# First-layer products of two neighbouring blocks in 512 columns, attention output in one PSUM bank instead of two

## The chip, the cores and the metric

The kernel runs on one core of a Trainium2 chip. The metric is the device time of one execution in microseconds (us). A core has five engines with a queue each: TensorE (PE in the profile, its weight loads PEld), VectorE (DVE), ScalarE (ACT), GpSimd (POOL) and SyncE (SP), which here issues most transfers. PSUM, into which TensorE writes, has eight banks of 128 partitions by 512 fp32 values.

## The reference

Three stages follow each other. A recurrent attention with decay makes 3072 rows of 384 values; a two-layer network with the same weights for all rows follows; then a routed layer with eight experts, which only rows with a positive skip score enter.

```python
f = 1 / (1 + exp(-f_logit))                       # 4 batches, 8 heads, 768 steps, 48 values
state = f[t] * state + outer(k[t], v[t])          # per head 48 x 48
y[t] = q[t] @ state
x = y.transpose(0, 2, 1, 3).reshape(3072, 384)
h = x @ w_in                                      # 384 x 2048
x = (h - tanh(h)) @ w_out                         # 2048 x 384
do = x @ w_skip > 0; e = argmax(x[do] @ w_gate)   # 8 experts, 384 x 1024 x 384
out = x; out[do] += gate * (relu(x @ w1[e]) @ w2[e])
```

## The kernel before, in words

**Units and blocks.** The rows are cut into 24 units of 128 rows (`u`: time chunk `c`, batch `b`); two units make a block of 256 rows (`blk`, 12 of them). `attend(u)` plans a unit's attention: `pl` (running sums of the decay, TensorE), `tk` and `tq` (transposes of k and q), `scores`, `mask` (DVE), `values`, the copies `out1` and `out2` (ACT), `renew` and `decay` of the state `S`. The transposed block then lies in `xT[blk]`, as a high part (`xhi`, ACT) and a low part (`xlo`, DVE). There are three such buffers (`AHEAD + 1`), and `xhi` of a block waits for the last first-layer product of the block three before (`lastG`).

**Attention on TensorE.** `scores` issues the 16 products `ps` of k and q (L511) and, for units 4 to 23, the 8 products of q with the state, which the code calls `recall` (L520). Heads come in four pairs `p` with two members `j`; member `j` has its state and its q on partitions 64j to 64j+47. The output `py` lies in two banks, one for each `j`. `side(p, j)` swaps the halves of the output for `p` of 2 and 3, so a recall of pair `p` and one of pair `p+2` use the four quarters of the 128 by 128 array between them: rows 0 or 64, columns 0 or 64. `values` adds the 8 products of the masked scores with v to `py` (L552) and makes the new state's part `pu` (L559). In the first chunk (units 0 to 3) the state is zero, and two products of 256 columns (L531) only set `py`.

**The two layers.** `gemm1(blk, f)` (step `G`) is one of 16 first-layer products of a block: nine matmuls of 128x256, three for each of three row groups (`whi` with both parts of x, `wlo` with the high part), L695. `tanh` (ACT, L702), `bend` (DVE, L707), `ghi` (ACT, L715) and `glo` (POOL, L721) follow, and `gemm2(blk, f)` (step `H`) adds six matmuls of 128x384 to the block's two accumulators `po` (L738). `H` stands two products behind `G` (`LAG`). After a block's last `H` its rows are copied out (`fin`), sent, and routed: nine dot products on DVE (L268), the choice, one small product `pp`, a scatter on POOL.

**What sets the order.** Blocks 0 to 9 are planned: every piece is a `Step` with an engine, a key, a cost and the PSUM buffers that it takes and gives. `in_order` lists the steps as a model of the engines would begin them, the first ones by the list `OPENING`, and they are emitted in that order, so each engine's queue is fixed. Blocks 10 and 11 are a hand-written loop of G, the routing steps, H. Eight experts close the program.

**PSUM before.** Four pools of two banks: `ph` (G's output), `po` (accumulators), `pa` (attention's short-lived tiles) and `yp` (both banks of `py`; block 1's accumulators too).

Of the kernel before, what the change touches and what calls it, by code (L numbers as in the profile page):

```python
# [97 lines left out]
def decay_attention_moe_kernel(  # L98
# [15 lines left out]
    P = 128  # L114
# [18 lines left out]
    FIRST, NJOIN, NPAY, SKEW = 6, 4, 6, 0  # L133
    EARLIEST, LEAD = -100, 32
# [284 lines left out]
    xT, xfs, dds = {}, {}, {}  # L419

    def side(p, j):

        return j if p < 2 else 1 - j
# [3 lines left out]
    def step(name, key, eng, cost, emit, *after, take=(), give=(), moved=0.0, lag=0.15):  # L427

        made[name] = x = Step(key, eng, cost, emit, after, take, give, moved, lag)
        steps.append(x)  # L430

    def attend(u):
# [13 lines left out]
        def at(pos):  # L446
            return (NF * blk - LEAD if u > FIRST - 1 else EARLIEST + 12 * blk) + 6 * half + pos
# [53 lines left out]

        def scores():
            kT, qT = m["kT"], m["qT"]
            ps = m["ps"] = [pa.tile([P, 512], F32, tag="pa", name=f"ps{u}_{j}") for j in range(2)]
            py = m["py"] = [yp.tile([P, 512], F32, tag="yp", name=f"py{u}_{j}") for j in range(2)]
# [10 lines left out]
            def recall(p):  # L516
                for j in range(2):
                    r = slice(64 * j, 64 * j + D)
                    o, w = 64 * side(p, j), (64, D)[side(p, j)]
                    nc.tensor.matmul(  # L520
                        py[j][o : o + w, p % 2 * P : p % 2 * P + P], lhsT=S[b][r, p, :w], rhs=qT[r, p],
                        start=(p % 2 == 0), stop=False,
                    )

            for p in range(2):
                score(p)
                if c:
                    recall(p)
                    recall(p + 2)
                else:  # L530
                    nc.tensor.matmul(  # L531
                        py[p][:64, : 2 * P], lhsT=S[b][:, 0].bitcast(BF16)[:, :64],
                        rhs=ones[:112, None, :].to_broadcast([112, 2, P]), start=True, stop=False,
                    )
                score(p + 2)
# [11 lines left out]
        def values():  # L547
            vt, py = loaded["v", u], m["py"]
            for p in range(NP):
                for j in range(2):  # L550
                    o = 64 * side(p, j)
                    nc.tensor.matmul(  # L552
                        py[j][o : o + D, p % 2 * P : p % 2 * P + P], lhsT=vt[:, 2 * p + j], rhs=m["A", j][:, p],
                        start=(c == 0 and o > 0 and p % 2 == 0), stop=(p % 2 == 1),
                    )
# [13 lines left out]

        def out1():  # L570
# [9 lines left out]
            py = m["py"]  # L580
            nc.scalar.activation(tm[:, half], py[1][:112, P : 2 * P], AF.Copy)
            nc.scalar.activation(xf[:112, 2, half], py[1][:112, :P], AF.Copy)

        def out2():
            nc.scalar.activation(
                xfs[blk][0][:112, :2, half], m["py"][0][:112, : 2 * P].rearrange("a (p t) -> a p t", p=2), AF.Copy
            )
# [34 lines left out]
        def xhi():  # L622
            x = xT[blk] = mpool.tile([P, KT, 2, 2 * P], F32R, tag="xT", name=f"xT{blk}", bufs=AHEAD + 1)
            nc.scalar.activation(x[:, :, 0], xfs[blk][0].rearrange("p k u t -> p k (u t)"), AF.Copy)
# [19 lines left out]
        step(("ck", u), at(1), "ACT", 0.59, copy4("k"), ("tk", u), ("scores", u - 2), give=((pk_in, f"k{u}"),))  # L644
        step(("tq", u), at(1.5), "PE", 0.44, turn4("q", qp4), ("mq", u), ("tk", u), take=((pk_in, f"q{u}"),), lag=0.25)
        step(("cq", u), at(1.5), "ACT", 0.59, copy4("q"), ("tq", u), ("scores", u - 2), give=((pk_in, f"q{u}"),))
        step(
            ("scores", u), at(2), "PE", 1.5 if c else 1.0, scores, ("ck", u), ("cq", u), ("decay", u - B), ("values", u - 1), 
            take=[("pa", f"s{u}{j}") for j in range(2)] + [("yp", f"y{u}{j}") for j in range(2)], lag=0.25,
        )  # L650
        for j in range(2):
# [4 lines left out]
        step(("values", u), at(3), "PE", 1.7 if u < FIRST else 1.3, values, ("mask", u, 1), ("v", u), take=(("pa", f"u{u}"),), lag=0.25)  # L656
        step(
            ("out1", u), at(3.5), "ACT", 0.6, out1, ("values", u), ("xlo", u - 1 - half) if blk > 1 else None, ("out2", u - 1),
            give=(("yp", f"y{u}1"),),
        )  # L660
        step(("out2", u), at(3.5), "ACT", 0.38, out2, ("out1", u), give=(("yp", f"y{u}0"),))
# [24 lines left out]
    po = {}  # L686

    def gemm1(blk, f):
        x = xT[blk]
        ph = ph_pool.tile([P, 2 * P], F32, tag="ph", name=f"ph{blk}_{f}")  # L690
# [6 lines left out]
        gt[blk, f] = ph  # L697
# [31 lines left out]
    def gemm2(blk, f, rows=(0, 1)):  # L729
        t = gt[blk, f]  # L730
        if f == 0:
            for s in range(2):
                home, tag, w = {1: (yp, "yp", 512)}.get(blk, (po_pool, "po", DM))
                po[blk, s] = home.tile([P, w], F32, tag=tag, name=f"po{blk}_{s}")[:, :DM]
        for s in rows:
            ss = slice(s * P, (s + 1) * P)
            for n, (a, w) in enumerate(((0, uhi), (0, ulo), (1, uhi))):
                nc.tensor.matmul(  # L738
                    po[blk, s], lhsT=t[:, a, ss], rhs=w[:, f], start=(f == 0 and n == 0), stop=(f == NF - 1 and n == 2)
                )  # L740
# [77 lines left out]
    def number():  # L818
        for at, n, begin in ((32, 32, (D * 7 - D + 32, 16)), (0, D, (0, 2 * D)), (96, 32, (D * 3 - 64 - D + 96, 16)), (64, D, (D * 4, 2 * D))):
            ids3 = rowid[at : at + n].rearrange("p (j i) -> p j i", i=KT)  # L820
            nc.gpsimd.iota(ids3, [[1, NWL], [NWL * begin[1], KT]], base=NWL * begin[0], channel_multiplier=NWL)
            if n == D:
                nc.gpsimd.iota(
                    ids3[:, :, KT - 1], [[1, NWL]], base=NWL * D * (1 if at else 5), channel_multiplier=NWL
                )
# [189 lines left out]
    def product2(g):  # L1015
        nonlocal routing
        blk, f = divmod(g - LAG, NF)
        first = (0,) if g - LAG >= NSLOT - SPLIT else (0, 1)
        gemm2(blk, f, first)
        if f == NF - 1:  # L1020
            finish(blk, first)
            if blk < NB - 1:
                for r in routing:
                    for _ in r:
                        pass
                routing = [late_route(2 * blk), late_route(2 * blk + 1)]
# [44 lines left out]
    for u in range(NU):  # L1071
        blk, half = divmod(u, 2)
        e = EARLIEST + 6 * u if u < FIRST else NF * blk - LEAD + 6 * half - 8
# [27 lines left out]
    slots = [(0, f) for f in range(NJOIN)] + [(1, f) for f in range(NJOIN - SKEW)]  # L1101
    for f in range(NJOIN, NF + SKEW):
        slots += [(b, f - SKEW * b) for b in range(2) if f - SKEW * b < NF]
    slots += [(b, f) for b in range(2, NB - AHEAD) for f in range(NF)]
    homes = {1: "yp"}
    for n, (b, f) in enumerate(slots):
        def do(fn, b=b, f=f):
            return lambda: fn(b, f)

        step(  # L1110
            ("G", n), n, "PE", 1.08, do(gemm1), ("xlo", 2 * b + 1), ("low", f // 2), ("G", n - 1), take=(("ph", f"g{n}"),), lag=0.25,
        )
        step(("T", n), n - 1000, "ACT", 0.39, do(tanh), ("G", n), ("glo", n - 2), ("ln", FIRST - 1))
        step(("bend", n), n - 1000, "DVE", 0.43, do(bend), ("T", n), give=(("ph", f"g{n}"),))
        step(("ghi", n), n - 1000, "ACT", 0.43, do(ghi), ("bend", n), ("H", n - LAG - 1))
        step(("glo", n), n - 1000, "POOL", 0.74, do(glo), ("ghi", n))
        if n == len(slots) - LAG:
            break_at = n
        if n < len(slots) - LAG:
            p = homes.get(b, "po")  # L1120
            step(
                ("H", n), n + LAG, "PE", 1.05, do(gemm2), ("glo", n), ("lou", f // 2), ("H", n - 1),
                ("values", FIRST - 1) if b in homes else None,
                take=[(p, f"o{b}{s}") for s in range(2)] if f == 0 else (), lag=0.25,
            )
            if f == NF - 1:
                for u in (2 * b, 2 * b + 1):
# [4 lines left out]
                    step(("out", u), n + LAG + 1, "SP", 0.45, (lambda u=u: finish2(u)), ("fin", u), moved=1.1)  # L1132
                    r = pieces(route(u))
# [10 lines left out]
        if f == NF - 1:  # L1144
# [10 lines left out]
    for g in range(NF * (NB - AHEAD), NSLOT + LAG):  # L1155
# [3 lines left out]
        for _ in range(3 if g >= NSLOT - NF else 2):  # L1159
# [412 lines left out]
```

## Time and profile before

| | |
|---|---|
| runs shown | 722.06, 721.72, 720.56 us; median 721.72 |
| the profiled execution | 720.9 us; span 718.9 us |
| TensorE busy | 691.1 us, 96% of the span, 6194 matmul records |
| VectorE, ScalarE, GpSimd busy | 68%, 51%, 42% |
| granted TensorE clock | 0.995 of full speed |
| chain that ended last | TensorE 75%, of it second-layer products 23%, first-layer products 23% |

A matmul's record holds its latency, so records overlap: what one matmul costs in a row of them is read from the distance between starts. An fp32 matmul of the attention leaves two records, one of the two layers (fp32r) leaves one. A row with "x8" is eight records that follow each other.

### The profile page before, as it was taken

The page shows a single profiled execution, that of the slowest core. Times are in us where ns is not written, and L with a number is a line of the kernel's source. Part 1 is how long each engine was busy: PE and PEld are TensorE (multiplying, and loading weights), DVE is VectorE, ACT ScalarE, POOL GpSimd, SP SyncE. Part 2 cuts the span into 40 slices and gives each one's busy share as a digit, 9 for nine tenths or more (in the row PEclk, how much of TensorE's full clock was granted, in tenths as well). Part 3 has the DMA queues.
Part 4 walks back from the last instruction along what each step waited for, and adds up shares of the span by engine and source line. Part 5 has one row for each costly group of instructions (what it writes and reads, how often), then busy time and mean ns, then how long its engine had stood idle before and what let it go on. Part 6 is the DMA issues. An engine that isn't in the chain of part 4 may idle for free.

```text
span 718.9 us, 16483 instructions
## 1 busy us (share of the span) xinstructions
PE 691.1 (96%) x6194; PEld 651.2 (91%) x6194; DVE 489.7 (68%) x1388; ACT 364.5 (51%) x882; POOL 300.5 (42%) x340
## 2 busy tenths in 40 slices
PE   7899989999999999999999999999999899999995
PEld 4578889999998999999999999999999789999995
DVE  3988987789669968668685774945585745555531
ACT  4867666546444564356546445444333435555530
POOL 4546444324244343443434344334443314555551
PEclk9999999999999999999999999999999999999998
DMA  9894345733121312312221220014002567666500
GB/s 221 224 258 133 116 170 144 253 75 63 46 45 48 72 34 72 58 50 46 63 62 29 59 44 14 24 59 157 6 35 91 192 216 232 216 214 215 175 16 24
DMA packets 147501, 76.75 MB, mean 107 GB/s; under 512 B 113288, under 2 KB 142617, under 8 KB 147286
## 3 DMA queue, kind: packets, MB, share of 16 engines
q1 hardware_dynamic: 142550, 64.18, 33.1%
q0 software_dynamic: 4768, 11.39, 4.5%
q8 instruction: 50, 0.82, 0.5%
q14 instruction: 37, 0.30, 0.1%
q10 hardware_dynamic: 96, 0.05, 0.0%
HBM read 61.60 MB, written 15.86 MB: 108 GB/s over the span
## 4 chain that ended last, share of the span: by engine, by line
PE 75%; DVE 9%; issue 5%; POOL 3%; ACT 3%; DMA 3%; SPq 0%; POOLq 0%; DVEq 0%; ACTq 0%
PE po L738 23%; PE ph L695 23%; PE eh L1224 8%; PE eo L1248 8%; PE ps L511 3%; DMA f<-in_f_logit_dram 3%; PE py L552 2%; POOL gs L721 2%; DVE scr L268 2%; PE eh L985 1%; PE pk L490 1%; PE py L520 1%; PE pu L559 1%; DVE th L707 1%; PE pq L490 1%
## 5 line engine op out<-in xcount | busy, mean ns | idle before, releaser
L721 POOL TENSOR_TENSOR gs<-th,gs 128x256 fp32r<-128x256 f32 x190 | 167.9, 887 | 233.6 <-ACT gs L715 214.7
L738 PE MATMUL po<-uhi,gs 128*128 128x384 f32 x768 | 232.3, 344 | 5.6 <-POOL gs L721 3.5
L695 PE MATMUL ph<-xT,whi 128*128 128x256 f32 x1152 | 219.7, 287 | 1.6 <-DVE th L707 1.3
L695 PEld LDWEIGHTS ph<-xT,whi 128*128 128x128 f32 x1152 | 184.2, 189 | 5.7 <-DVE th L707 2.8
L695 PE MATMUL ph<-xT,wlo 128*128 128x256 f32 x576 | 162.6, 282 | 0.0
L738 PEld LDWEIGHTS po<-uhi,gs 128*128 128x128 f32 x768 | 142.0, 189 | 12.0 <-POOL gs L721 6.4
L707 DVE TENSOR_TENSOR th<-ph,th 128x256 f32<-128x256 f32 x192 | 79.8, 418 | 85.2 <-ACT th L702 84.8
L268 DVE CUSTOM_DVE_ANT_0 scr<-pay,wb 128x384 f32<-128x384 f32 x198 | 128.8, 650 | 7.9 <-ACT pay L746 4.1
L715 ACT ACTIVATE gs<-th 128x256 fp32r<-128x256 f32 x192 | 79.5, 416 | 102.9 <-DVE th L707 100.5
L738 PE MATMUL po<-ulo,gs 128*128 128x384 f32 x384 | 129.2, 336 | 0.0
L702 ACT ACTIVATE th<-ph 128x256 f32<-128x256 f32 x192 | 72.4, 379 | 102.0 <-PE ph L695 66.9
L695 PEld LDWEIGHTS ph<-xT,wlo 128*128 128x128 f32 x576 | 109.4, 190 | 0.0
L738 PEld LDWEIGHTS po<-ulo,gs 128*128 128x128 f32 x384 | 73.1, 190 | 0.0
L1224 PE MATMUL eh<-xt,w 128*128 128x256 f32 x504 | 69.8, 283 | 0.0
L1248 PE MATMUL eo<-w,h 128*128 128x384 f32 x336 | 69.5, 342 | 0.0
L1224 PEld LDWEIGHTS eh<-xt,w 128*128 128x128 f32 x504 | 67.1, 188 | 0.4
L1248 PEld LDWEIGHTS eo<-w,h 128*128 128x128 f32 x336 | 56.5, 188 | 0.0
L1233 DVE SCALAR_TENSOR_TENSOR h<-eh,h 128x256 fp32r<-128x256 f32 x56 | 23.7, 422 | 46.1 <-ACT h L1232 46.1
L1232 ACT ACTIVATE h<-eh 128x256 fp32r<-128x256 f32 x56 | 21.5, 385 | 62.6 <-PE eh L1224 62.5
L780 POOL DMA_INDIRECT xs<-pay,dst x24 | 25.1, 1046 | 64.2 <-DVE sm L280 21.2
L352 POOL TENSOR_TENSOR w<-r,w 128x768 fp32r<-128x768 f32 x24 | 44.3, 1853 | 12.7 <-ACT w L351 12.7
L957 POOL DMA_INDIRECT out_dram<-yo,xa x16 | 15.9, 992 | 68.2 <-DVE yo L965 22.1
(194 smaller groups left out, 933.2 us busy)
## 6 DMA issues: line engine op xcount, KB each, us to landing
r<-in_moe_w_dram SPq DMA_DIRECT2D x56, 384.0 KB, 4.7
stgu<-in_moe_w_out_dram SPq DMA_DIRECT2D x4, 1536.0 KB, 6.3
f<-in_f_logit_dram SPq DMA_DIRECT2D x24, 192.0 KB, 3.3
out_dram<-pay SPq DMA_DIRECT2D x24, 192.0 KB, 3.5
k<-in_k_dram SPq DMA_DIRECT2D x22, 192.0 KB, 3.5
q<-in_q_dram SPq DMA_DIRECT2D x22, 192.0 KB, 3.1
v<-in_v_dram SPq DMA_DIRECT2D x22, 192.0 KB, 4.4
xs<-zrow SPq DMA_DIRECT2D x2, 1544.0 KB
```

The costliest lines, as they stand in the source:

```text
L268: nc.vector.tensor_tensor_reduce(out=scr, in0=x, in1=wb[:, n], scale=1.0, scalar=0.0, op0=ALU.mult, op1=ALU.add, accum_out=lg[:, n : n + 1])
L352: eng.tensor_tensor(lo, raw, hi.bitcast(F32), ALU.subtract)
L695: nc.tensor.matmul(ph, lhsT=w[:, i, fs], rhs=x[:, i, a], start=(n == 0), stop=(n == 3 * KT - 1))
L702: nc.scalar.activation(th, ph, AF.Tanh)
L707: nc.vector.tensor_tensor(th, ph, th, ALU.subtract)
L715: nc.scalar.activation(t[:, 0], th, AF.Copy)
L721: eng.tensor_tensor(t[:, 1], th, t[:, 0].bitcast(F32), ALU.subtract)
L738: nc.tensor.matmul(po[blk, s], lhsT=t[:, a, ss], rhs=w[:, f], start=(f == 0 and n == 0), stop=(f == NF - 1 and n == 2))
L780: nc.gpsimd.indirect_dma_start(xs[:, :], bass.IndirectOffsetOnAxis(ap=di, axis=0), pt[:, :], None, bounds_check=E * NT - 1, oob_is_err=False,)
L1224: nc.tensor.matmul(ph, lhsT=a1[:, w, i, f * P : (f + 1) * P], rhs=xt[:, i, a], start=(n == 0), stop=(n == 3 * KT - 1))
L1233: nc.vector.scalar_tensor_tensor(out=h[:, 1], in0=ph, scalar=0.0, in1=h[:, 0].bitcast(F32), op0=ALU.max, op1=ALU.subtract)
L1248: nc.tensor.matmul(eo[e, s], lhsT=h[:, a, ss], rhs=a2[:, w, f], start=(f == 0 and n == 0), stop=(f == NF2 - 1 and n == 2))
```

## The change

- From block 2 to block 9, a first-layer product is made for two neighbouring blocks at once: the nine matmuls have 512 columns, 256 of each block, and one weight load serves both. Blocks are offset by half a width: block 2 makes its products 0 to 7 alone, blocks 2 and 3 share 8 to 15, 3 and 4 share 0 to 7, and so on up to 8 and 9, and block 9 makes 0 to 7 alone. The order is the list `slots`, the partner stands in `mate`. 56 shared products take the place of 112, and 16 stay single.
- Two blocks are then open at a time, so the accumulators of the odd blocks 1 to 9 lie in the two banks of `yp`. For units from 6 on, `py` is one bank, taken from `pa` when `values` begins; `recall` moves from `scores` to the head of `values`, and `side` goes: a member's output lies on the partitions 64j for all four pairs. In units 4 and 5 `recall` stays in `scores`.
- `out1` and `out2` are two copies (112x128 and 112x384) where three were. Units 0 to 3 set `py` by one product of 512 columns. `number` has two index fills fewer.
- The three buffers of `xT` become one tile, units from 6 on are planned up to eight products earlier (`begun`), H of a shared product stands 3.2 behind (`LAG2`), and routing of units 17 to 19 goes to the loop of blocks 10 and 11, with three routing steps for each product where two were in block 10.

```diff
+    LAG2 = 3.2
-    def side(p, j):
-        return j if p < 2 else 1 - j
+    xall = mpool.tile([P, AHEAD + 1, KT, 2, 2 * P], F32R, tag="xT", name="xall", bufs=1)
+    xT = [xall[:, b % (AHEAD + 1)] for b in range(NB)]
+    half_f = (range(NF // 2), range(NF // 2, NF))
...
+    slots += [(2, f) for f in half_f[0]]
+    for b in range(2, LASTB):
+        for f in half_f[(b - 1) % 2]:
+            slots += [(b, f), (b + 1, f)]
+            mate[b, f] = mate[b + 1, f] = (b, b + 1)
+    slots += [(LASTB, f) for f in half_f[(LASTB - 1) % 2]]
...
+    def begun(u):
+        blk, half = divmod(u, 2)
+        return NF * blk - LEAD + 6 * half - (NF // 2 if 2 < blk <= LASTB else 0)
...
+        def recall(p):
+            for j in range(2):
+                r = slice(64 * j, 64 * j + D)
+                w = (64, D)[j]
+                nc.tensor.matmul(
+                    m["py"][64 * j : 64 * j + w, p * P : (p + 1) * P], lhsT=S[b][r, p, :w], rhs=m["qT"][r, p],
+                    start=(p == 0), stop=False,
+                )
...
         def values():
+            if u >= FIRST:
+                m["py"] = pa.tile([P, 512], F32, tag="pa", name=f"py{u}")
+                for p in range(NP):
+                    recall(p)
...
-            nc.scalar.activation(tm[:, half], py[1][:112, P : 2 * P], AF.Copy)
-            nc.scalar.activation(xf[:112, 2, half], py[1][:112, :P], AF.Copy)
+            nc.scalar.activation(tm[:, half], m["py"][:112, KT * P :], AF.Copy)
...
+    homes = {b: "yp" for b in range(1, LASTB + 1, 2)}
     def gemm1(blk, f):
-        x = xT[blk]
-        ph = ph_pool.tile([P, 2 * P], F32, tag="ph", name=f"ph{blk}_{f}")
+        if (blk, f) in mate:
+            s = sorted(b % (AHEAD + 1) for b in mate[blk, f])
+            x = xall[:, s[0] : s[1] + 1 : s[1] - s[0]].rearrange("p b i a t -> p i a b t")
+            both = ph_pool.tile([P, 2, 2 * P], F32, tag="ph", name=f"ph{blk}_{f}")
...
                 nc.tensor.matmul(ph, lhsT=w[:, i, fs], rhs=x[:, i, a], start=(n == 0), stop=(n == 3 * KT - 1))
...
-        for _ in range(3 if g >= NSLOT - NF else 2):
+        for _ in range(3):
             route_step()
```

**TensorE's queue, attention of unit 20, before.** In these rows `ps` are the scores and `py` the recall; 64x128 and 48x128 are the output's partitions and columns.

```order
L511 MATMUL ps_0_5970<-qT_5953,kT_5924 64x128
L511 MATMUL ps_1_5971<-qT_5953,kT_5924 64x128
L520 MATMUL py_0_5972<-qT_5953,S_108 64x128
L520 MATMUL py_1_5973<-qT_5953,S_108 48x128
L520 MATMUL py_0_5972<-qT_5953,S_108 48x128
L520 MATMUL py_1_5973<-qT_5953,S_108 64x128
L511 MATMUL ps_0_5970<-qT_5953,kT_5924 64x128
L511 MATMUL ps_1_5971<-qT_5953,kT_5924 64x128
```

Both members of two head pairs stand together, each tile `py_0` and `py_1` in a bank of its own, in both halves.

**The same queue, unit 20, with the change.** This is the head of `values`; `A` are the masked scores and `ph` a shared first-layer product.

```order
L729 MATMUL ph_6_5466<-xall,wlo 128x512
L524 MATMUL py_5479<-qT_5402,S_108 64x128
L524 MATMUL py_5479<-qT_5402,S_108 48x128
...
L576 MATMUL py_5479<-A_0_5461,v_4762 48x128
L576 MATMUL py_5479<-A_1_5464,v_4762 48x128
...
L583 MATMUL pu_5496<-v_4762,kp_112 64x48 x8
```

The recall has left the scores and stands between a product of the layers and the products with `A`, in the order j=0, j=1 for each of the four pairs: always rows 0 with columns 0 and rows 64 with columns 64.

**The same queue, blocks 7 and 8, with the change.** `ph_2` and `ph_3` are shared products, `po_0_5226` is an accumulator of block 8 and `po_0_4751` one of block 7.

```order
L729 MATMUL ph_2_5206<-xall,whi 128x512 x2
L729 MATMUL ph_2_5206<-xall,wlo 128x512
...
L771 MATMUL po_0_5226<-uhi,gs_0_5168 128x384
L771 MATMUL po_0_5226<-ulo,gs_0_5168 128x384
...
L771 MATMUL po_0_4751<-uhi,gs_1_5202 128x384
L771 MATMUL po_0_4751<-ulo,gs_1_5202 128x384
...
L729 MATMUL ph_3_5252<-xall,whi 128x512 x2
```

Where one G and one H took turns, one shared G is followed by two H: block 8's of the product two shared ones back, and block 7's of the one just before.

## Rows read from the trace of the kernel before

**Rows 1.** The page: span, TensorE's busy time, the chain's shares.
```profile
span 718.9 us, 16483 instructions
PE 691.1 (96%) x6194; PEld 651.2 (91%) x6194; DVE 489.7 (68%) x1388; ACT 364.5 (51%) x882; POOL 300.5 (42%) x340
PE 75%; DVE 9%; issue 5%; POOL 3%; ACT 3%; DMA 3%; SPq 0%; POOLq 0%; DVEq 0%; ACTq 0%
```

**Rows 2.** Busy time by stretch: window, length, PE, PEld, DVE, ACT, POOL, granted clock, DMA share, GB/s.
```profile
0.00:130.00 130.00, 117.16 (x1122) 101.05 (x1123) 103.40 (x176) 86.59 (x196) 63.89 (x98) 0.99 0.67 182
130.00:230.00 100.00, 98.26 (x1038) 92.38 (x1037) 79.98 (x263) 49.67 (x132) 36.59 (x45) 1.00 0.33 82
230.00:500.00 270.00, 269.13 (x2603) 258.22 (x2602) 192.00 (x635) 134.91 (x353) 108.49 (x126) 1.00 0.24 57
500.00:560.00 60.00, 58.56 (x416) 57.31 (x415) 36.47 (x150) 23.39 (x65) 24.91 (x28) 1.00 0.17 57
```

**Rows 3.** Waits of TensorE from 130 to 500: total us, times, longest.
```profile
PE po L738 <- POOL gs L721: 1.8, 3, 0.9
```

**Rows 4.** Timeline, TensorE at 500 us: start, length, line, tiles, shape, records.
```profile
500.07 0.40 PE L695 MATMUL ph<-xT,whi 128*128 128x256 f32 x2
...
501.14 0.34 PE L738 MATMUL po<-uhi,gs 128*128 128x384 f32 x1
...
502.19 0.40 PE L695 MATMUL ph<-xT,whi 128*128 128x256 f32 x2
```

**Rows 5.** Lines by form, TensorE, first expert's second products: busy us, mean ns.
```profile
L994 PE MATMUL eo<-r,h 128*128 128x384 f32 x32 | 10.7, 486 | 0.0
```

**Rows 6.** Timeline, TensorE, the scores of unit 20, around 406 us.
```profile
405.93 0.34 PE L738 MATMUL po<-uhi,gs 128*128 128x384 f32 x1
406.19 0.45 PE L511 MATMUL ps<-qT,kT 48*64 48x128 f32 x8
406.46 0.40 PE L520 MATMUL py<-qT,S 48*64 48x128 f32 x8
406.68 0.62 PE L511 MATMUL ps<-qT,kT 48*64 48x128 f32 x16
...
407.34 0.40 PE L511 MATMUL ps<-qT,kT 48*64 48x128 f32 x8
407.67 0.50 PE L695 MATMUL ph<-xT,whi 128*128 128x256 f32 x2
408.01 0.28 PE L695 MATMUL ph<-xT,wlo 128*128 128x256 f32 x1
```

**Rows 7.** Timeline, TensorE, the values of unit 20, around 410 us.
```profile
409.98 1.08 PE L552 MATMUL py<-A,v 128*48 128x128 f32 x16
410.89 0.62 PE L559 MATMUL pu<-v,kp 128*64 128x48 f32 x16
411.44 0.50 PE L695 MATMUL ph<-xT,whi 128*128 128x256 f32 x2
```

**Rows 8.** Timeline, TensorE, scores of a unit of the first chunk.
```profile
19.59 0.30 PE L531 MATMUL py<-ones,S 112*64 112x256 bf16 x1
19.82 0.67 PE L511 MATMUL ps<-qT,kT 48*64 48x128 f32 x16
20.42 0.30 PE L531 MATMUL py<-ones,S 112*64 112x256 bf16 x1
```

**Rows 9.** Lines by form, ScalarE's copies of `py`: busy us, mean ns, idle before.
```profile
L585 ACT ACTIVATE xf<-py 112x256 f32<-112x256 f32 x22 | 8.4, 382 | 0.0
L582 ACT ACTIVATE xf<-py 112x128 f32<-112x128 f32 x22 | 6.0, 270 | 0.1
L581 ACT ACTIVATE tm<-py 112x128 f32<-112x128 f32 x22 | 5.9, 268 | 3.4 <-PE py L552 3.3
```

**Rows 10.** Timeline, TensorE, the longest of these waits.
```profile
220.25 0.34 PE L738 MATMUL po<-ulo,gs 128*128 128x384 f32 x1
221.51 0.62 PE L738 MATMUL po<-uhi,gs 128*128 128x384 f32 x2 [0.92 <-POOL gs L721]
```

More of the change, by code (lines that the diff above doesn't have):

```diff
@@ L504, in scores @@
             ps = m["ps"] = [pa.tile([P, 512], F32, tag="pa", name=f"ps{u}_{j}") for j in range(2)]
-            py = m["py"] = [yp.tile([P, 512], F32, tag="yp", name=f"py{u}_{j}") for j in range(2)]
+            if u < FIRST:
+                m["py"] = yp.tile([P, 512], F32, tag="yp", name=f"py{u}")
             def score(p):
@@ L514, in score @@
                         )
[L516 to L523, printed above, removed]
             for p in range(2):
                 score(p)
-                if c:
+                if u >= FIRST:
+                    pass
+                elif c:
                     recall(p)
                     recall(p + 2)
-                else:
+                elif p == 0:
                     nc.tensor.matmul(
-                        py[p][:64, : 2 * P], lhsT=S[b][:, 0].bitcast(BF16)[:, :64],
-                        rhs=ones[:112, None, :].to_broadcast([112, 2, P]), start=True, stop=False,
+                        m["py"][:64], lhsT=S[b][:, 0].bitcast(BF16)[:, :64],
+                        rhs=ones[:112, None, :].to_broadcast([112, NP, P]), start=True, stop=False,
                     )
@@ L655, in attend @@
             )
-        step(("values", u), at(3), "PE", 1.7 if u < FIRST else 1.3, values, ("mask", u, 1), ("v", u), take=(("pa", f"u{u}"),), lag=0.25)
         step(
-            ("out1", u), at(3.5), "ACT", 0.6, out1, ("values", u), ("xlo", u - 1 - half) if blk > 1 else None, ("out2", u - 1),
-            give=(("yp", f"y{u}1"),),
-        )
-        step(("out2", u), at(3.5), "ACT", 0.38, out2, ("out1", u), give=(("yp", f"y{u}0"),))
+            ("values", u), at(3), "PE", 1.7, values, ("mask", u, 1), ("v", u), ("decay", u - B) if u >= FIRST else None,
+            take=[("pa", f"{x}{u}") for x in ("u" if u < FIRST else "yu")], lag=0.25,
+        )
+        step(
+            ("out1", u), at(3.5), "ACT", 0.3, out1, ("values", u), ("xlo", u - 1 - half) if blk > 1 else None, ("out2", u - 1),
+        )
+        step(("out2", u), at(3.5), "ACT", 0.52, out2, ("out1", u), give=(("yp" if u < FIRST else "pa", f"y{u}"),))
         old = [("decay", 2 * blk - 4), ("decay", 2 * blk - 3), ("in_range", 2 * blk - 3)]
@@ L738, in gemm2 @@
                 nc.tensor.matmul(
-                    po[blk, s], lhsT=t[:, a, ss], rhs=w[:, f], start=(f == 0 and n == 0), stop=(f == NF - 1 and n == 2)
+                    po[blk, s], lhsT=t[:, a, ss], rhs=w[:, f], start=(f == first_f[blk] and n == 0),
+                    stop=(f == last_f[blk] and n == 2),
                 )
@@ L1098, in decay_attention_moe_kernel @@
         attend(u)
[L1101 to L1106, printed above, removed]
+    NSTEP = NF * (LASTB + 1)
+    for n, (b, f) in enumerate(slots[:NSTEP]):
         def do(fn, b=b, f=f):
             return lambda: fn(b, f)
+        m = mate.get((b, f), (b,))
+        if m[0] == b:
+            step(
+                ("G", n), n, "PE", 1.07 if len(m) == 1 else 2.04, do(gemm1), *[("xlo", 2 * w + 1) for w in m], ("low", f // 2),
+                ("G", n - 1), take=(("ph", f"g{n}"),), lag=0.25,
+            )
+            held = n
+        else:
+            made["G", n] = made["G", n - 1]
+        step(("T", n), n - 1000, "ACT", 0.39, do(tanh), ("G", n), ("glo", n - 2), ("ln", FIRST - 1))
@@ L1110, in decay_attention_moe_kernel @@
         step(
-            ("G", n), n, "PE", 1.08, do(gemm1), ("xlo", 2 * b + 1), ("low", f // 2), ("G", n - 1), take=(("ph", f"g{n}"),), lag=0.25,
-        )
-        step(("T", n), n - 1000, "ACT", 0.39, do(tanh), ("G", n), ("glo", n - 2), ("ln", FIRST - 1))
-        step(("bend", n), n - 1000, "DVE", 0.43, do(bend), ("T", n), give=(("ph", f"g{n}"),))
+            ("bend", n), n - 1000, "DVE", 0.43, do(bend), ("T", n), ("bend", n - 1) if held < n else None,
+            give=(("ph", f"g{held}"),) if m[-1] == b else (),
+        )
```

77 lines of the change are left out of this document (42 added, 35 removed).

## The prediction

> **What bounds the kernel now.** I read the page first: TensorE is busy 96% of the span and carries 75% of the chain that ended last [rows 1]. Then the windows: from 130 to 560 us TensorE is busy 98 to 100% at full granted clock, with DVE at 61 to 80% [rows 2]; before 130 it is busy 90% and transfers and ScalarE share the bound. Then TensorE's waits in the bound part: the only ones of size are 1.8 us for GpSimd's low parts, from 130 to 500 [rows 3]. So what this change does to attention and to the layers after 130 us is worth what it does to TensorE's own work, nearly one to one. A busy TensorE need not be efficient, so I took what a matmul costs from distances between starts, not from record lengths.
>
> The sum is made against the profiled execution: 720.9 us, of which the span is 718.9 and 2.0 lie outside. The median of the runs shown, 721.7, is 0.8 above it.
>
> **Shared products.** Nine matmuls of 256 columns stand between 500.07 and 501.14, so 118.9 ns each; six of 384 columns between 501.14 and 502.19, 175.0 ns each [rows 4]. The change makes 56 x 9 = 504 matmuls of 512 columns from 1008 of 256. No such matmul is in the trace. Upper end of its price: twice the short one, 237.8 ns, which saves nothing. A line through the two rows gives 175.0 + 56.1 = 231.1 ns, a saving of 6.7 ns each or 3.4 us. At the 2.4 GHz level one column a cycle would be 106.7 and 160.0 ns, so the rows carry 12.2 and 15.0 ns on top; their middle on 213.3 ns gives 227 ns. I take 227, since it is nearest to both rows: 10.9 ns x 504 = **5.5 us saved**. Lower end of the price: the 384-column matmuls of the first expert, fp32 and not fp32r, come in two runs of 16 and take (10.7 - 2 x 0.486) / 30 = 324 ns from start to start [rows 5], two cycles a column (320) and only 4 ns on top. If long streams lose their overhead like that, 512 columns take 217 ns and 20.8 ns x 504 = 10.5 us are saved. The ends are 0 and 10.5.
>
> The Trainium skill (TensorE: Matmul & The Clock Gate, Back-to-back issue gap) gives N/2.4 + 2.5 ns for a warm matmul of N columns, 109 ns at 256 and 216 at 512; by it alone sharing would save 2.5 ns x 504 = 1.3 us. The trace's 118.9 ns [rows 4] contradicts its first value.
>
> **Recall loses two of its four tiles.** In the scores, recall records come four at a time: eight of them take 0.22 us (406.46 to 406.68), 0.11 us for each four, and 16 of the scores behind them take 0.44 [rows 6]. A unit has 16 recall records, so it pays 0.44 us. The four of a group are on the four quarters of the array, which is what `side` was for. Without it only two quarters are used, rows 0 with columns 0 and rows 64 with columns 64. How two tiles go is shown by the products of the masked scores with v, which use two column halves: 16 records in 0.91 us (409.98 to 410.89), 0.11 us for each two [rows 7]. So 16 recall records will take eight times 0.11, 0.88 us: 0.44 us more, for 18 units **7.9 us more**. The lower end is 0, if two tiles ran as fast as four; nothing in the rows says so. In this part of the program no other engine's wait covers it: in the order a shared product or two H stand between a unit's scores and its values, long enough for the masks.
>
> **One more change of tile shape.** At the head of `values` recall (64 by 64 tiles) now meets the products with `A` (all 128 rows). No row shows that pair, but others price such a change. From the last `po` to the first `ps` there are 0.26 us against a cadence of 0.175, and the first eight `ps` take 0.27 where eight take 0.22 [rows 6]. The last eight `ps` take 0.33 before `ph`, 0.11 over, and the next two `ph` 0.34 against 0.24. The best pair is in the first chunk: an L531 in the midst of the scores takes 0.23 us, where 256 columns at one a cycle are 0.107, and the 16 scores behind it 0.60 instead of 0.44, so going there and back costs 0.28 [rows 8]. I take half of that, 0.14 us, for one change: x 18 = **2.5 us more**, with ends of 0.09 x 18 = 1.6 and 0.25 x 18 = 4.5. The scores themselves keep one entry and one exit, as before, and so do the values.
>
> The Trainium skill (TensorEngine Tiling (Array Packing), Key Properties) says that a change of tiling mode drains TensorE while a change of tile within a mode doesn't. It speaks against this change, which puts a mode change inside `values`. The trace bears that out for other pairs [rows 6, 8]; by it the term stands, without it the sum would be 2.5 us lower.
>
> **Waits.** The two longest waits of the bound part stand where block 2 begins, the longest 0.92 us at 221 us [rows 10]: before, units 6 to 9 were held until block 1 had left the two `yp` banks, and then came packed into ten products. Now `py` no longer needs `yp`, units 6 and 7 run in the last products of blocks 0 and 1, and 8 to 11 spread over block 2. Also, one shared product of about 2 us and two H now stand between a product and the H that needs its low part, so GpSimd has more room. I take **1.0 us less** of the 1.8 [rows 3]. What is late next: `py` now shares the two `pa` banks with `pu`, and the next unit's `pl` and `tk` take those banks, so they wait for `out2` (ACT) and `renew` (DVE). In the order two H, 2.1 us, stand between; the copies take about 0.27 + 0.48 us, so I count nothing. If that cover went, each unit would lose up to 0.5 us.
>
> **ScalarE and the opening.** `out1` and `out2` were 268 + 270 + 382 ns [rows 9]; the new pair is 268 and, by the step of 112 ns for each 128 columns, 494 ns: 0.16 us less a unit. After 130 us ScalarE is half idle [rows 2], so that is covered by TensorE. In the opening six units save 1.0 us on ScalarE, and four units save one L531 with its two changes, 0.28 us each, on TensorE [rows 8]; units 4 and 5 pay 0.44 us of recall each. All lies partly behind transfers. I take **0.5 us less**, between 2 less and 1 more. The two index fills are short GpSimd work before the first transfers and are in that.
>
> **Edits that I count at nothing.** The added routing steps in block 10: nine dot products, the choice and five `bend` steps go into five products' time, and DVE has been doing just this beside block 11, where 500 to 560 us show DVE at 61% and TensorE at 98% [rows 2]. The offset blocks keep one `fin` in every 16 products, with more room before the bank is needed again. One weight load for two blocks: loads lie beside matmuls in any case.
>
> **Sum.** -5.5 + 7.9 + 2.5 - 1.0 - 0.5 = +3.4 us: 724.3 on the profiled execution's terms, 725.1 on the median's. **I forecast 725.0 us**, slower by 0.5%. For its own terms the range is 721 to 729.
>
> **Rivals.**
> - *Long matmuls lose their overhead* (the other side: faster). A shared matmul takes 217 ns by the expert's measure [rows 5], in all 56 products: -10.5 + 7.9 + 2.5 - 1.5 = -1.6, or 720.1. It decides from 18 ns saved on each matmul, (7.9 + 2.5 - 1.5) / 504, that is below 220 ns. For it: the 4 ns of the long fp32 matmuls. Against: overhead grows from 12.2 to 15.0 ns between 256 and 384 columns. The Trainium skill's N/2.4 + 2.5 (the page and section above) would give 216 ns.
> - *Recall costs what it did.* If two tiles are as fast as four, or its time falls into a wait, the sum is -5.5 + 2.5 - 1.5 = -4.5, 717.2. Against: 0.11 us for two tiles [rows 7].
> - *Sharing saves nothing*: 238 ns each. Then +7.9 + 2.5 - 1.5 = +8.9, 730.6. For it: weight loads lie beside the matmuls, 91% and 96% busy [rows 1], so there may be nothing to remove.
> - *The two `pa` banks become a wait* of 0.5 us a unit: 18 x 0.5 on top of the forecast, 734. Against: 2.1 us of cover.
>
> That the change doesn't do what it says is excluded by the order: 504 rows of 128x512 are there, and all recalls stand in `values`.
>
> **How the numbers follow.** Forecast 0.50, long matmuls 0.17, recall unchanged 0.10, no saving 0.14, banks 0.09. The 0.2% that a measurement can tell is 1.4 us: faster is below 720.3, slower above 723.2. Faster: half of the second (0.09), the third (0.10) and a tail of the first (0.02), 0.21. Same: the rest of the second (0.08) and the low part of the first (0.13), 0.21. Slower: 0.58. The range for 8 in 10 runs from 718 to 731: it leaves out most of the third case and the fifth.
>
> **What would show it.** Right: starts of the 128x512 matmuls about 227 ns apart, a shared product in about 2.04 us; recall's 16 records in about 0.9 us, in twos; about 0.1 us lost between recall and the products with `A`; TensorE still busy 98% from 130 on; waits for GpSimd near 221 us gone. Wrong: under 220 ns between those starts, recall in fours, or TensorE idle for `out2` or `renew` before `pl` and `tk`.

## The result, and the profile after

The change is **slower**: 729.41 us median of 6 runs (727.46 to 730.11) beside 721.14 (719.08 to 722.19) for the kernel before on the same chip, a ratio of 1.0111, 95% interval 1.0089 to 1.0133. A second set on one chip (the experiment `again` below) gave 727.71 beside 722.48, 1.0078 (1.0063 to 1.0094). I forecast +3.3 us; the two sets measure +8.3 and +5.2.

The page of the changed kernel, against [rows 1]:

```profile
span 728.1 us, 15460 instructions
PE 701.0 (96%) x5686; PEld 633.5 (87%) x5686; DVE 497.1 (68%) x1388; ACT 359.6 (49%) x858; POOL 301.2 (41%) x338
PE 76%; DVE 6%; issue 5%; POOL 2%; ACT 1%; DMA 0%; ACTq 0%; POOLq 0%; DVEq 0%
```

There are 508 fewer records of matmuls, 504 of them by the sharing, and yet TensorE is busy 9.9 us longer. It is the bound as before, so the time has to be looked for in its own instructions. By stretch, against [rows 2] (window, length, PE, PEld, DVE, ACT, POOL, granted clock, DMA share, GB/s):

```profile
0.00:130.00 130.00, 117.58 (x1149) 100.21 (x1150) 103.80 (x173) 84.03 (x184) 63.73 (x94) 0.96 0.65 176
130.00:230.00 100.00, 98.44 (x921) 87.53 (x920) 76.37 (x239) 49.47 (x128) 32.89 (x40) 1.00 0.39 95
230.00:500.00 270.00, 269.25 (x2121) 237.50 (x2120) 188.19 (x609) 128.04 (x328) 107.52 (x126) 1.00 0.22 53
500.00:560.00 60.00, 59.55 (x428) 58.47 (x427) 47.65 (x184) 24.74 (x72) 30.34 (x34) 1.00 0.08 26
```

From 130 to 560 us TensorE is busy 98% and more at full clock, as it was. The waits for GpSimd's low parts [rows 3] are gone from this list; what stands there now (TensorE, 130 to 500: total us, times, longest) is the transposes of k and q and the scores, each waiting for an operand from DVE or ScalarE:

```profile
PE pk L508 <- DVE kp L495: 1.2, 4, 0.7
PE ps L539 <- ACT qT L515: 0.6, 2, 0.5
PE pq L508 <- DVE qp L498: 0.4, 1, 0.4
```

The timeline of TensorE around unit 20 answers to [rows 4, 6, 7] (start, length, line, tiles, shape, records):

```profile
412.22 1.10 PE L539 MATMUL ps<-qT,kT 48*64 48x128 f32 x32
413.25 0.45 PE L771 MATMUL po<-uhi,gs 128*128 128x384 f32 x1
...
415.45 0.63 PE L729 MATMUL ph<-xall,whi 128*128 128x512 f32 x2
...
417.30 0.40 PE L729 MATMUL ph<-xall,wlo 128*128 128x512 f32 x1
417.62 1.08 PE L524 MATMUL py<-qT,S 48*64 48x128 f32 x16
418.64 1.08 PE L576 MATMUL py<-A,v 128*48 128x128 f32 x16
419.55 0.62 PE L583 MATMUL pu<-v,kp 128*64 128x48 f32 x16
```

The eight steps from 415.45 to 417.30 are (417.30 - 415.45) / 8 = 0.231 us each: a 512-column matmul. The recall takes 1.02 us from its start to the first product with `A`, where the forecast had 0.88 + 0.14. The products with `A` still take 0.91 us.

Before the experiments I made an account that no single view gives. Call the sixteen G of a block its first products and the sixteen H its second ones. Take the stretch from the first matmul of the 17th second product of the program (block 0's ninth) to the first second product of block 10: 144 first and 144 second products and the 18 units from 6 on lie in it in every kernel, so the work is the same but for one unit's small routing products. Each matmul is charged the time until the next one starts, waits included. These sums are mine, from the starts in the traces; the kernels beside before and after are those of the experiments:

```
us                 before  after  again   attn alone4 share4  late4
first products      162.0  155.9  155.8  161.7  162.6  155.1  155.9
second products     160.9  163.8  163.8  162.2  162.5  164.3  161.8
recall                7.9   18.3   18.3   18.3   11.2   10.8   10.8
A times v, new state 27.3   26.3   26.3   26.3   26.3   26.3   26.3
scores               18.6   18.6   18.6   18.6   18.6   18.6   18.6
transposes           12.6   13.3   13.3   12.7   13.3   12.7   13.0
log-decay, routing    8.4    7.1    7.1    7.2    7.2    7.2    7.1
stretch             397.6  403.3  403.2  407.0  401.7  395.0  393.4
opening up to it     92.9   96.0   92.3   97.8   94.7   96.5   95.8
to the last matmul  219.4  219.9  220.2  219.4  219.7  219.4  221.6
```

In the stretch the change costs 5.7 us, in both of its profiles. One part of that comparison is not the kernel's: in the one profile of before the granted clock stands at the lower of its two levels for a part of this stretch, near 102 us, while the six other profiles of the table have the full clock in all of it. Before's trace shows it in the busy times from 99 to 105 us (granted clock 0.72, columns as above) and in the second products that stand there:

```profile
99.00:105.00 6.00, 5.63 (x26) 5.31 (x27) 5.97 (x9) 3.67 (x9) 2.20 (x3) 0.72 0.48 194
...
102.42 0.52 PE L738 MATMUL po<-uhi,gs 128*128 128x384 f32 x1
102.74 0.52 PE L738 MATMUL po<-ulo,gs 128*128 128x384 f32 x1
103.06 0.84 PE L738 MATMUL po<-uhi,gs 128*128 128x384 f32 x2
```

Matmuls that elsewhere start 0.175 us apart start 0.32 us apart here, and the first product ahead of them takes 2.08 us (100.34 to 102.42) instead of some 1.1. That is about 1.5 us, an estimate from these distances, so at full clock the change's stretch costs some 7.2 us. The opening is another matter: 3.1 us later than before in the first profile and 0.6 us earlier in the second.

### The profile page after: what moved, and what is told of

Same layout as the page of the kernel before. It is cut to its first block, busy times and chain, and to the rows that moved or that the text cites. A ratio compares the mean times of both kernels' runs of the same rounds, so it can differ in the third digit from the quotient of the medians.

```text
span 728.1 us, 15460 instructions
## 1 busy us (share of the span) xinstructions
PE 701.0 (96%) x5686; PEld 633.5 (87%) x5686; DVE 497.1 (68%) x1388; ACT 359.6 (49%) x858; POOL 301.2 (41%) x338
## 4 chain that ended last, share of the span: by engine, by line
PE 76%; DVE 6%; issue 5%; POOL 2%; ACT 1%; DMA 0%; ACTq 0%; POOLq 0%; DVEq 0%
PE po L771 23%; PE ph L729 23%; PE eh L1257 8%; PE eo L1281 8%; PE ps L539 3%; PE py L524 3%; PE py L576 2%; POOL gs L754 2%; PE eh L1015 1%; PE pu L583 1%; PE pk L508 1%; PE pq L508 1%; DVE w L353 1%; PE eo L1024 1%; DVE xall L650 1%
## 5 line engine op out<-in xcount | busy, mean ns | idle before, releaser
L754 POOL TENSOR_TENSOR gs<-th,gs 128x256 fp32r<-128x256 f32 x190 | 165.7, 878 | 230.8 <-ACT gs L748 220.7
L729 PE MATMUL ph<-xall,whi 128*128 128x256 f32 (+1 forms) x816 | 198.9, 333 | 2.4 <-DVE th L740 1.1
L729 PEld LDWEIGHTS ph<-xall,whi 128*128 128x128 f32 x816 | 139.4, 190 | 16.0 <-DVE th L740 2.2
L269 DVE CUSTOM_DVE_ANT_0 scr<-pay,wb 128x384 f32<-128x384 f32 x198 | 134.9, 681 | 7.1 <-ACT pay L780 3.1
L729 PE MATMUL ph<-xall,wlo 128*128 128x256 f32 (+1 forms) x408 | 134.7, 330 | 0.0
L740 DVE TENSOR_TENSOR th<-ph,th 128x256 f32<-128x256 f32 x192 | 76.5, 417 | 71.9 <-ACT th L735 71.5
L735 ACT ACTIVATE th<-ph 128x256 f32<-128x256 f32 x192 | 68.5, 379 | 105.6 <-PE ph L729 74.8
L729 PEld LDWEIGHTS ph<-xall,wlo 128*128 128x128 f32 x408 | 77.8, 191 | 6.9
L814 POOL DMA_INDIRECT xs<-pay,dst x24 | 28.8, 1198 | 62.0 <-DVE dst L813 44.5
```

The source lines that it names most:

```text
L269: nc.vector.tensor_tensor_reduce(out=scr, in0=x, in1=wb[:, n], scale=1.0, scalar=0.0, op0=ALU.mult, op1=ALU.add, accum_out=lg[:, n : n + 1])
L729: nc.tensor.matmul(ph, lhsT=w[:, i, fs], rhs=x[:, i, a], start=(n == 0), stop=(n == 3 * KT - 1))
L735: nc.scalar.activation(th, ph, AF.Tanh)
L740: nc.vector.tensor_tensor(th, ph, th, ALU.subtract)
L754: eng.tensor_tensor(t[:, 1], th, t[:, 0].bitcast(F32), ALU.subtract)
L814: nc.gpsimd.indirect_dma_start(xs[:, :], bass.IndirectOffsetOnAxis(ap=di, axis=0), pt[:, :], None, bounds_check=E * NT - 1, oob_is_err=False,)
```

## The experiments

My theory after the comparison: in the stretch, recall at two quarters of the array and in its new place costs what was forecast, the shared products give back less than was forecast, and the opening lost 3 us more because the granted clock fell there. The rivals: the order that sharing forces, or the scarce `pa` banks, cost the time; or the single bank for `py` does.

All levels "at equal clock" below come from one fit: a level for each kernel, and one slope on the mean granted clock, over the 145 executions of all these runs; the slope is 0.29 us for each 0.001, and the levels are taken at .993. Their standard errors are 0.2 us for before (722.4, 58 executions) and 0.4 to 0.6 us for the others.

### share4: sharing, but recall over four quarters again

```diff
+                m["py"] = [pa.tile([P, 512], F32, tag="pa", name=f"py{u}_{j}") for j in range(2)]
+                for p in (0, 2, 1, 3):
+                    recall(p)
-            pu = m["pu"] = pa.tile([P, 512], F32, tag="pa", name=f"pu{u}")
+            pu = m["pu"] = py[1][:, 2 * P :] if u >= FIRST else pa.tile([P, 512], F32, tag="pa", name=f"pu{u}")
```

`side`, the recall's target `py[j]` with its two column places, and the copies of `py` are those of before.

> The shared 512-column products stay as in the change; the two-bank attention takes the rows of before again, so that its recall of units 6 and later runs over four quarters of the array (order of pairs 0, 2, 1, 3) into two pa banks, with the new state's product in the spare columns of the second; the opening's units are those of before. Theory (the recall at two tiles at a time is most of the loss): against the change minus 18 x 0.44 = 7.9 us in the recall, and the opening back at the clock it had, minus 2 to 3 us: 718.5 to 722, a recall of about 0.45 us plus its entry. Rival (the loss lies in the order of the shared products and the scarce pa banks, not in the recall): no nearer to before than 727.

Measured: 721.10 beside 722.32, ratio 0.9977 (0.9962 to 0.9992); 720.7 at equal clock, 7.5 below the mean of the change's two levels (728.5 and 728.0). In its trace 16 recall records take 0.59 us up to the first product with `A`, instead of 1.02:

```profile
411.56 0.67 PE L529 MATMUL py<-qT,S 48*64 48x128 f32 x16
412.15 1.08 PE L582 MATMUL py<-A,v 128*48 128x128 f32 x16
```

18 x 0.43 = 7.7 us, and the account's recall row falls by 7.5 (18.3 to 10.8). So nearly the whole loss is the recall's, and sharing with this recall is a little faster than before. The time fell into the expected range partly by luck: the expectation counted 2 to 3 us for the opening, and share4's opening (96.5 us) is no earlier than the change's (96.0). But share4 changes quarters and banks together: each half of the heads now has its own bank.

### share2: the same, with the pairs in the order 0, 1, 2, 3

```diff
-                for p in (0, 2, 1, 3):
+                for p in range(NP):
```

> The same as share4 in every instruction, only the pairs of the recall stand in the order 0, 1, 2, 3, so that two neighbours use the same two quarters. Theory: the recall takes 0.87 us instead of 0.44, 18 units, so share4 plus 7.9 us: 726.5 to 730. Rival (the recall of units 6 and later is priced by its place behind the masks, not by the quarters): within 1 us of share4.

Measured: 720.48, ratio 0.9976 (0.9959 to 0.9993). The expectation from the theory was wrong by the whole 8 us:

```profile
410.59 0.68 PE L529 MATMUL py<-qT,S 48*64 48x128 f32 x16
411.20 1.08 PE L582 MATMUL py<-A,v 128*48 128x128 f32 x16
```

0.61 us, as with the other order; the rival's time came true. The fault was in the experiment: over the unit each of the four quarters still gets two products, whatever the order. The first four records of the recall start within 33 ns of each other here (20 ns in share4), so a product that finds its quarter busy doesn't hold up the next one for a free quarter. What counts is then how much each quarter has to do, or else the bank; share2 can't tell these apart.

### halves2: two quarters, but two banks

```diff
-                m["py"] = pa.tile([P, 512], F32, tag="pa", name=f"py{u}")
+                m["yh"] = [pa.tile([P, 512], F32, tag="pa", name=f"py{u}_{j}") for j in range(2)]
...
-                    pu[64 * j : 64 * j + 64, p * D : (p + 1) * D], lhsT=kp[:, h], rhs=vt[:, h], start=True, stop=True
+                    (pu if u < FIRST else py[1 - j])[64 * j : 64 * j + 64, p * D : (p + 1) * D], lhsT=kp[:, h], rhs=vt[:, h],
+                    start=True, stop=True
```

> The change, but from unit 6 on the values' first half of heads lies in one pa bank and the second half in the other (still two quarters of the array, each with its own bank; the new state's product in the free halves of both; four copies and two sums where there were two and one). It tells quarters from banks. Theory (a quarter does one product after the other, so two quarters take 0.87 us for a recall where four take 0.43): a recall of about 1.0 us with its entry as in the change, 728 to 730. Rival (two halves that write one bank hinder each other): a recall of 0.6 us as in share4 and share2, 720.5 to 722.

Measured: 730.47 beside 722.48, ratio 1.0114 (1.0093 to 1.0134). The recall takes 1.02 us, as in the change:

```profile
416.08 1.08 PE L524 MATMUL py<-qT,S 48*64 48x128 f32 x16
417.10 1.08 PE L577 MATMUL py<-A,v 128*48 128x128 f32 x16
```

So it is the quarters. With two in use, each does four products one after the other. The 2 us above the change are not the recall's; this kernel has two more copies and one more sum in each unit, on ScalarE and DVE. TensorE's waits from 130 to 500 us are 3.7 us in its list against 2.2 in the change, which makes 1.5 of these 2 us; what each copy costs was not tried by itself. The fourth corner, four quarters in one bank, was not tried either.

### attn: the change without its sharing

```diff
-    slots += [(2, f) for f in half_f[0]]
...
+    slots += [(b, f) for b in range(2, NB) for f in range(NF)]
-    homes = {b: "yp" for b in range(1, LASTB + 1, 2)}
+    homes = {1: "yp"}
```

So `mate` stays empty and every product is a single one.

> The change without its sharing: blocks in the order of before, one product of 256 columns for each, the attention in two pa banks with the recall in two tiles. Theory: 504 products of 512 columns at 231 ns against 1008 of 256 at 118.5 ns saved 3 us, so this is the change plus 3 us: 731.5 to 734. Rival (sharing saved nothing, or its order cost what it saved): 728 to 730, or less.

Measured: 732.37, ratio 1.0127 (1.0101 to 1.0152); 731.6 at equal clock, so the change's sharing is worth 3.3 us (731.6 less 728.25). The account agrees: 407.0 to 403.3 in the stretch, first products 5.8 us less, second ones 1.6 more, transposes 0.6 more. Without the sharing the attention alone costs 9.4 us of the stretch as charged, and 9.2 at equal clock (731.6 less 722.4).

### alone4: share4 without its sharing

The edit is that of attn, made to share4.

> share4 without the sharing: blocks and products of 256 columns as in before, the recall of units 6 and later in four quarters but behind the masks, in two pa banks. It closes the square with before, share4, attn and the change. Theory: the sharing saves 3.0 us here as it did with the other attention (attn against the change), so share4 plus 3 us, 723.5 to 724.5 at the clock of the first set; and the recall's new place costs 1 us against before by its two changes of tile shape. Rival (the gain of sharing needs the attention's order, or the place costs nothing): 721 to 722.5.

Measured: 727.04 beside 722.48, ratio 1.0068 (1.0047 to 1.0088); 727.1 at equal clock. It closes the square: sharing is worth 6.4 us here, twice the 3.3 of the other column, so neither the expected 3 us nor the rival held. TensorE's waits from 130 to 500 us are the larger in alone4, 4.3 us in the list:

```profile
PE pl L481 <- DVE A L559: 1.3, 1, 1.3
PE po L773 <- POOL gs L756: 1.0, 3, 0.6
PE pk L506 <- DVE kp L493: 1.0, 1, 1.0
PE ps L537 <- ACT qT L513: 0.7, 1, 0.7
PE po L773 <- ACT pay L782: 0.3, 1, 0.3
```

and 2.6 us in share4 (the first three lines of its list stand at late4 below), 2.2 in attn and in the change. So some 1.7 us of the difference between the columns are waits that this order happens to meet; what makes up the rest stays open (the standard error of the difference of the two is 0.9). The recall's new place can be read off as well: against before, four quarters in both, recall is 3.3 us dearer and the products with `A` 1.0 cheaper, 2.3 us for 18 units, 0.13 a unit. Of that 0.45 us is a single unit, whose recall took 1.04 us where the others took 0.60; in share4, where none does, the place costs 1.9 us, 0.10 a unit. I had expected 1 us here, and 2.5 in the prediction.

### fill: work in the opening's gap

In the profile of the change the granted clock is 0.74 between 50 and 70 us, against 1.00 before and in `again`:

```profile
50.00:70.00 20.00, 18.42 (x197) 17.09 (x192) 12.54 (x25) 14.13 (x30) 9.32 (x11) 0.74 0.55 141
```

Ahead of it TensorE waits three times (in brackets: us, and for what):

```profile
50.95 0.67 PE L583 MATMUL pu<-v,kp 128*64 128x48 f32 x16 [0.38 <-ACT kT L515]
52.64 0.38 PE L729 MATMUL ph<-xall,whi 128*128 128x256 f32 x1 [0.59 <-ACT xall L646]
53.63 0.58 PE L729 MATMUL ph<-xall,whi 128*128 128x256 f32 x1 [0.61 <-DVE xall L650]
```

```diff
+            for _ in range(12 if u == 4 else 0):
+                nc.tensor.matmul(pu[:, 3 * P :], lhsT=ones, rhs=ones, start=True, stop=True)
```

> The change with twelve products of ones by ones (128 columns, bf16) behind unit 4's values, at the place (52 us) after which the granted clock stood at half for 10 us. They add work and compute nothing that is used. Theory (the opening's 3 us are the clock's): no half clock near 53 us, mean granted clock .995 instead of .989 to .991, 726.5 to 728 us. Rival (the opening is late for another reason, such as the single bank for the values): 729 to 730 whatever the clock does.

Measured: 728.99, ratio 1.0080 (1.0058 to 1.0102); 728.8 at equal clock, as the change, and a mean clock of .993 over its six runs, where the change had .991 and then .994. Its own profile still has 0.93 up to 50 us and 0.91 from 50 to 70. So the filler cured nothing that can be measured. Ten of the twelve profiles kept show the lower clock somewhere between 10 and 105 us, at different places; `again` and lag4 do not.

### again: the change once more

No edit.

> The changed kernel once more, word for word, beside the two others of this set on one chip. Theory: the clock of the opening differs from execution to execution in every kernel (some .34 us for each .001 of the mean granted clock over the first 59 executions), and at an equal clock the change costs 6 us: 1.007 to 1.010 of before. Rival (the opening of the change itself loses 3 us): 1.011 or more, with a mean clock below that of before by .003.

Measured: 727.71 beside 722.48, ratio 1.0078 (1.0063 to 1.0094), mean clock .994. In its profile the same stretch of the opening has full clock, and the span is 724.6 instead of 728.1:

```profile
50.00:70.00 20.00, 17.89 (x213) 16.25 (x212) 16.12 (x28) 15.32 (x32) 11.68 (x12) 1.00 0.58 149
```

So the opening of the change is not slower by itself. The first six runs had a lower clock than these six, and the runs of before beside them (721.14) lay lower than the 58 of before in the later sets (medians 722.32, 722.48 and 721.31). At equal clock the two sets give 728.5 and 728.0 against 722.4: the change costs **some 6 us** (5.9, standard error 0.4). The profiles say a little more, 7.2 in the stretch at full clock and 0.6 less in the opening of `again`, but before left one profile alone, and its run (720.9) lay below the 722.4 of its kind.

### late4, lag4, share4b: a version that beats both

The largest waits left in share4 stand ahead of `pk` (TensorE, 130 to 500 us):

```profile
PE pk L513 <- DVE kp L500: 1.5, 4, 1.0
PE pl L488 <- DVE A L566: 0.9, 1, 0.9
PE ps L544 <- ACT qT L520: 0.2, 1, 0.2
```

late4 lets the planner reckon with a later DVE, lag4 moves the second product of a shared pair, and share4b is share4 unchanged:

```diff
-        step(("mk", u), at(1), "DVE", 0.56, mk, ("ek", u), ("k", u))
+        step(("mk", u), at(1), "DVE", 0.56, mk, ("ek", u), ("k", u), lag=0.15 if u < FIRST else 1.2)
...
-    LAG2 = 3.2
+    LAG2 = 2.2
```

> share4 with one rule of the planner changed: the products that scale k and q (mk, mq) are given 1.2 us instead of 0.15 before their transposes may be planned, from unit 6 on, so that a product of the network stands ahead of the transpose while VectorE is still late (waits of 1.33, 0.51, 0.51 and 0.50 us ahead of pk in share4, at 209, 298, 341 and 254 us). Theory (TensorE is the bound, so a wait removed is a time saved): minus 1.5 to 2.5 us against share4. Rival (the transposes then stand later, and the banks they hold make the next unit wait as long): within 1 us of share4.

> share4 with the second product of a shared pair planned 2.2 places behind the first instead of 3.2. Theory: waits of po for gs come back, 56 pairs x 0 to 0.05 us: share4 plus 0 to 3 us. Rival (the products behind a pair wait less for the pa banks): minus 1 us.

> share4 once more, beside the two variants on one chip: .9977 of before within .002, and below before where the variants do not beat it. Rival: its gain over before was the luck of the first set's openings, and it is within .001 of before.

Measured, beside 721.31 (24 runs): late4 717.58, ratio 0.9928 (0.9902 to 0.9953); lag4 721.91, 1.0004 (0.9982 to 1.0026); share4b 720.11, 0.9973 (0.9952 to 0.9995). The 1.33 us of late4's expectation was read from start to start; 1.0 of it is idle time, the longest of the list above. late4's list for the same stretch:

```profile
PE pk L513 <- DVE kp L500: 0.3, 2, 0.2
PE ps L544 <- ACT qT L520: 0.2, 1, 0.2
```

2.1 us of waits are gone, and the stretch is 1.6 us shorter (395.0 to 393.4). At equal clock late4 is at 717.7, 2.8 below share4's two sets (720.7 and 720.4, standard error of the difference 0.5), and the fastest kernel here; by the medians it is 2.5 us below share4b, the far end of its theory's range. Its profiled run is the slowest of its seven, 721.48 us, with 2.2 us more than share4 behind block 10's start, where the granted clock fell to the lower level (0.72 from 575 to 581 us, 1.00 in share4). So the 1.6 of the stretch are shown by the trace and the other 1.2 us by the levels alone. lag4 is 1.8 us slower than share4b, within its theory's range; waits for low parts come back, but at four places and not at 56:

```profile
PE po L780 <- POOL gs L763: 1.9, 4, 0.5
```

share4's gain over before held a second time.

## Why the prediction was wrong in size

The direction, the mechanism and its main price were right. Two terms of the sum were mis-sized, the saving by the shared products, which was taken at 5.5 us and is 3.1, and the waits, which were to fall by 1.0 us and did not fall. They outweigh the attention, which was priced 1.0 us too high, and so a change of some 6 us was forecast as one of 3.3; the first set lay another 2 us above that by its draw.

- **Recall at two quarters: +7.9 forecast, 7.5 measured** (18.3 against 10.8 in share4, alike but for the quarters). halves2 excludes the bank as its cause. The rival that recall costs what it did is out: 16 records take 1.02 us.
- **The change of tile shape: +2.5 forecast, 1.9 to 2.3 measured** (share4 and alone4 against before). The Trainium skill (TensorEngine Tiling (Array Packing), Key Properties) says that tiles work independently and that a change of mode drains the engine. share2, where the order of the pairs made no difference (0.61 us against 0.59), agrees with the first, and these 0.10 to 0.13 us a unit are in line with the second. That the new place costs this much is measured; no run here separates the change of shape from the rest of the move.
- **The shared products: -5.5 forecast. This is the term that failed.** A 512-column matmul starts 231 ns after the one before it, not 227: the line through the two rows [rows 4] was exact, and moving the price toward the mean overhead was not justified by any row. At positions 2 to 8 of the nine, at full clock, two short ones take 237.2 ns on average in before's stretch (and in attn's), and a long one 231.1 in the change's (231.2 in share4's), so the cadence saves 504 x 6.1 = 3.1 us, where the line gave 3.4. attn against the change gives 3.3 us for sharing as a whole, with a standard error of 0.6, and 3.7 in the stretch. In the account the first products' row falls by more, 6.1 us, and the second products' row rises by 2.9. Before's low clock is in both rows, with some 1.0 and 0.6 us. Most of the rest is a shift: 57 of the 144 second products stand right behind a piece of attention, where 29 did, and their first matmul then takes 0.25 to 0.28 us instead of 0.175. "Long matmuls lose their overhead" is out, for over 256, 384 and 512 columns the distance grows by 56 ns a step. By the formula of the Trainium skill (TensorE: Matmul & The Clock Gate, Back-to-back issue gap), which holds there for isolated matmuls and not for a stream of weight loads and matmuls like this one, 512 columns would take 216 ns; the trace's 231 lies above it, as 118.9 lay above its 109 at 256.
- **The waits: -1.0 forecast, -0.2 measured in the lists from 130 to 500 us (2.4 to 2.2), +0.3 as TensorE's idle time in the stretch (4.1 to 4.4).** This term failed too. The waits for GpSimd went as told, that of [rows 10] among them. But waits of 2.2 us for DVE and ScalarE came, ahead of `pk`, `pq` and `ps`. I had looked at whether `out2` and `renew` free a bank in time; the waits came from an operand instead, k times its decay, which DVE finishes late. "The two `pa` banks become a wait" is out as priced: the wait is 1.2 us in 4 units, not 9 in 18.
- **The opening: -0.5 forecast; between -0.6 and +3.1 in the two profiles.** What the change does there is below what one execution differs from the next.
- **ScalarE's copies: as told**, 0.16 us less a unit, and TensorE covers it. The two lines by form (busy us, mean ns) answer to [rows 9]:

```profile
L607 ACT ACTIVATE xf<-py 112x384 f32<-112x384 f32 x22 | 10.6, 484 | 0.0
L604 ACT ACTIVATE tm<-py 112x128 f32<-112x128 f32 x22 | 6.0, 274 | 16.8 <-PE py L576 16.7
```

So of the 8.3 us of the first set some 6 are the change's. The sum missed 2.4 us of them at the price of the long matmul (5.5 less 3.1) and 0.8 to 1.3 at the waits, and had the attention 1.0 too dear (recall and products with `A` together: +9.4 in the account, 10.4 forecast). With these three set right, +3.4 becomes 5.6 to 6.1. For the stretch alone, without the opening, the same terms give up to 6.6 of the 7.2 at full clock; what the rest is stays open. The remaining 2 us are the draw of that set: its runs of before lay 1.2 us below the level of before, and the change's 0.9 above its own.

## What to carry to other kernels

Price a longer matmul by the line through the shorter ones in the trace; a price below it needs a row that shows the gain. Where small products are laid over parts of the array, count what each part has to do: with two quarters in use instead of four the recall took 1.02 us instead of 0.59, whether the two wrote one bank or two, and this outweighed a saving on far larger matmuls. Look at the granted clock of the stretch in both profiles before two sums of them are subtracted. When one half of a two-part change pays and the other costs, look for a layout that keeps only the first: here the spare columns of a second bank held what had needed a bank of its own.

## What was not expected of the hardware

- A product whose quarter is busy does not hold up later products for free quarters: 0.61 us for the pairs in the order 0, 1, 2, 3 and 0.59 for 0, 2, 1, 3.
- Products from the two halves of the rows can write one bank at the same time, each to its own partitions: in the change the records of such a pair start 7 to 8 ns apart, and the recall takes 1.02 us, as with a bank for each half (halves2).
- The granted clock of the opening fell in some executions and not in others of the same kernel: 0.74 from 50 to 70 us in one profile of the change and 1.00 in the other, with spans 3.5 us apart. One execution's opening can't be read as the kernel's.
